# Attention weights of batches 2 and 3 turned on VectorE through DRAM, with a new order on every engine

## The chip, the cores and the metric

One core of one Trainium2 chip runs the program. The metric is device time in microseconds (us), the median of three runs of one kernel. A profile is one more execution, taken by the hardware profiler; its span runs from the first instruction to the last. Engines: PE is TensorE, DVE is VectorE, ACT is ScalarE, POOL is GpSimd, SP is SyncE, which issues every DMA here.

## The reference

Attention over chunks of 32 queries, each against 8 memory keys and a window of at most 56 keys, and behind it a gated feed-forward layer:

```python
# 4 batches, 8 heads, 768 tokens, head size 64; chunk 32, left 16, right 8, 8 memory keys
scores = scale * np.matmul(q_c, k_full.transpose(0, 1, 3, 2))      # k_full: memory keys and window
a = np.exp(scores - max); a = a / (np.sum(a, axis=-1, keepdims=True) + 1e-09)
out[:, :, c_start:c_end] = np.matmul(a, v_full)
# then x = out, tokens x 512
h = np.maximum(x @ w_in, 0.0)                                      # 1024 wide
conv_out = conv_w[0] * h[t - 1] + conv_w[1] * h[t] + conv_w[2] * h[t + 1]
return (h / (1.0 + np.exp(-conv_out))) @ w_out
```

The weights w_in, conv_w and w_out come as float64.

## The kernel before

**Work.** Attention runs in 32 steps, 8 for each batch: half of the tokens (384) by a pair of heads. A step loads q, k and v (L471); PE makes the scores s (L481, 12 fp32 matmuls that the trace shows as 24 records); DVE takes the maximum and subtracts it (L397, L402) or ACT does so inside the exponential (L423); ACT takes exp (L435); DVE sums (L448) and inverts (L455); DVE or POOL normalises (L459). Then PE turns the weights e with three 128x128 matmuls against the identity into a bank t (L502), ACT copies t in two halves into the one block-diagonal tile a_d (L513), and PE multiplies with v into a bank a (L521, 24 records). ACT rounds a into x_hi (L530) and DVE keeps the rest as x_lo (L533). A step's x is a quarter of one half of the feed-forward's input.

**Feed-forward.** Every fp32 product there is three fp32r matmuls, hi by hi, hi by lo, lo by hi. ffn_in (L556) makes h in 16 half rows for each batch, each of 4 quarters by 3 matmuls of 384 columns. The gate takes h through one tap on ACT or DVE (L583, L587), two on DVE (L593), a sigmoid on ACT (L597) and a product on DVE or POOL (L601); split makes g hi on ACT (L611) and g lo on DVE or POOL (L614). ffn_out (L632) makes 6 tiles of 128 tokens for each batch, each of 8 rows of g by 3 matmuls of 512 columns, and ACT copies the bank out (L644). The float64 weights are taken apart into hi and lo by chains of eight or so operations on DVE, ACT and POOL (L289 to L363).

**Two shapes on PE.** Scores and values (L481, L521) use the array in 64x64 pieces, here called tiled; all else uses the whole array. A switch is a change from one to the other.

**Order.** Nothing runs in the order of the code. `Plan` collects operations with a cost, a due number and dependences, and `run` issues them as a list scheduler would, among those ready first the one with the smallest due (L161). Each engine then runs its own list in that fixed order, and an instruction that waits holds up all behind it on its engine; the DMAs stand in one list on SP. The due numbers are straight lines, `lin(name, i)`, out of the table DUE; a switch is charged 12.1 in the choice (L162) and 95 or 120 ns in the cost (L176). Strings such as MULT, LO, NORM and ZADD, one letter for each step or row, say which of V (DVE), G (POOL) and A (ACT) does an operation; in W_IN and W_OUT a small letter puts the first maximum of a weight's chain on POOL (L293).

**PSUM.** Eight banks: two for s, one t, one a, four f, which both ffn_in and ffn_out use.

Of the kernel before, what the change touches and what calls it, by code (L numbers as in the profile page):

```python
# [9 lines left out]
F32 = mybir.dt.float32  # L10
# [12 lines left out]
NH = 2  # L23
# [5 lines left out]
W64 = 4  # L29
# [3 lines left out]
W_IN, W_OUT = "CRScCmcc", "McCCMcmm"  # L33
# [3 lines left out]
TAP = "AAAAAAAAAAAAAAVVAAAAAAAAAVVVVAAA"  # L37
MULT = "VVVGGGGGGVGGGGGGGGVGGVGVVGGGGVVV"
LO = "VGVVVVVGGVVVVVGGVVVGGGGVVVGGVVVV"
SOFT = "VVAVVVVVVVABABAAAVVVVVABBBVVAVAB"  # L40
NORM = "GGGGGGGGVVGGGGGGGGGGGGGGVGVVVGVV"
ZADD = "VGGGGVGGGGGVGGVGGVVVVGGGVGGVVVVV"
GROUP = "11111111"

DUE = {
    "early": (1.3, 2.83), "qk0": (-13.5, 0.8), "v0": (104.5, 0), "late": (-19.1, 0), "w_in": (-14.7, 2.93),
    "w_in_load": (-18.2, 4.91), "w_out": (78.5, 2.37), "w_out_load": (4.1, 15.21), "load": (-130.9, 0),
# [4 lines left out]
    "gate": (29.9, 2.03)  # L52
# [3 lines left out]
class Tile:  # L56


    def __init__(self, ring, make):
        self.ring, self.make, self.t, self.left, self.due = ring, make, None, 0, None  # L60


class Plan:
# [11 lines left out]
    def op(self, eng, cost, due, do, r=(), w=(), shared=False, table=None, mode=None, late=70):  # L75
# [24 lines left out]
        self.ops.append((eng, cost, due, do, after - {i}, tiles, shared, table, mode, late))  # L100
# [10 lines left out]
    def run(self):  # L111
# [13 lines left out]
        free, shared_free, queue_free = defaultdict(float), 0.0, 950.0  # L125
# [9 lines left out]
        for _ in range(n):  # L135
            best = None
            for e, c in cand.items():
                at = []
# [32 lines left out]
            eng, cost, due, do, after, tiles, shared, tab, md, late = ops[i]  # L171
# [42 lines left out]
SWITCH, MODE = 100.2, 12.1  # L214
# [3 lines left out]
def attention_then_gated_ffn(  # L218
# [39 lines left out]
    a_d = const.tile([P, NG * 4, 2, CH], F32, name="a_d")  # L258
    nc.gpsimd.memset(a_d, 0.0)
# [5 lines left out]

    def lin(name, i):
        return DUE[name][0] + DUE[name][1] * i

    def from_f64(src, hi, lo, key, n, kind, due, first):
# [9 lines left out]
        def op(eng, cost, do, r, wr, **kw):  # L281
# [90 lines left out]
    def attention(steps, due, soft, norm, zadd):  # L372


        ns = len(steps)
# [80 lines left out]
        for i, n in enumerate(steps):  # L456
# [17 lines left out]
    def scores(s, q_d, k_t, due):  # L474
# [14 lines left out]
        plan.op("PE", 24 * 30, due, mm, (q_d, k_t), (s,), mode="tiled", late=250)  # L489

    def outcome(n, v_t, e, i, due):
# [3 lines left out]
        t, a = bank("t", 1), bank("a", 1)  # L495
# [4 lines left out]
        def turn():  # L500
            for g in range(NG):
                nc.tensor.transpose(  # L502
                    out=t.t[:, g * P : (g + 1) * P],
                    in_=e.t[:, i, 2 * g : 2 * g + 2].rearrange("p g k -> p (g k)"),
                    identity=ident,
                )
# [294 lines left out]
```

## Time and profile before

| what | value |
| --- | --- |
| time, median of 3 runs (lowest to highest) | 360.23 us (359.33 to 361.78) |
| span of the profiled execution | 357.6 us |
| PE busy | 341.4 us, 95% of the span |
| DVE busy | 244.7 us, 68% |
| ACT busy | 240.4 us, 67% |
| POOL busy | 125.2 us, 35% |
| DMA read, written | 41.84 MB, 6.29 MB |

Matmuls overlap, so a record's length is not what it costs: the step from one start to the next is. A busy share over the whole span mixes stretches with different limits.

### The profile page before, as it was taken

The numbers are of one execution on the slowest core, as the hardware profiler recorded it, in microseconds if no ns is written. First come the engines' busy times: TensorE is split into PE (matmuls) and PEld (weight loads), VectorE is DVE, ScalarE is ACT, GpSimd is POOL, SyncE is SP. The second block draws the span as 40 slices with busy tenths as digits, with TensorE's granted clock in tenths as the row PEclk, the third lists the DMA queues.
The fourth block names the chain that finished last, engine by engine and source line by source line (L and its number), as shares of the span: only waits on it lengthen the run. The fifth ranks groups of instructions, "written<-read, shape, count | busy, mean of one in ns | idle before, by whom it ended". The sixth has DMA issues, their size and how long they took to land.

```text
span 357.6 us, 7589 instructions
## 1 busy us (share of the span) xinstructions
PE 341.4 (95%) x3000; PEld 302.1 (84%) x3000; DVE 244.7 (68%) x408; ACT 240.4 (67%) x492; POOL 125.2 (35%) x167
## 2 busy tenths in 40 slices
PE   1699999999999999999999999999999999999996
PEld 1588899999899987778888899997878799998886
DVE  3899898988889998779933026889644128998000
ACT  4468588878679999887979158877466345675101
POOL 2376554442373253774572003354010002560000
PEclk9989999999999999999999999999999999999999
DMA  7999961969623146134416200006272000000111
GB/s 267 402 387 311 383 234 63 341 208 283 209 95 116 25 139 227 68 104 152 129 44 250 88 31 0 2 0 188 80 294 75 30 31 2 0 0 3 59 59 61
DMA packets 19909, 48.63 MB, mean 136 GB/s; under 512 B 2337, under 2 KB 6689, under 8 KB 19873
## 3 DMA queue, kind: packets, MB, share of 16 engines
q1 hardware_dynamic: 19872, 48.14, 39.0%
q8 instruction: 24, 0.39, 0.5%
q14 instruction: 13, 0.10, 0.1%
HBM read 41.84 MB, written 6.29 MB: 135 GB/s over the span
## 4 chain that ended last, share of the span: by engine, by line
PE 69%; DVE 10%; DMA 5%; ACT 5%; POOL 5%; issue 4%; SPq 1%; POOLq 0%; DVEq 0%; ACTq 0%
PE f L632 33%; PE f L556 24%; PE a L521 5%; PE s L481 5%; DVE c L593 3%; PE t L502 2%; DMA h<-in_k_dram 2%; POOL c L601 2%; DMA w<-in_w_out_dram 2%; ACT c L597 2%; DMA w<-in_w_in_dram 2%; POOL w_top L293 2%; DVE z L448 1%; DVE w_top L299 1%; DVE top L397 1%
## 5 line engine op out<-in xcount | busy, mean ns | idle before, releaser
L632 PE MATMUL f<-w_out_hi,g 128*128 128x512 f32 (+1 forms) x400 | 127.6, 391 | 0.2 <-ACT o_sb L644 0.2
L556 PE MATMUL f<-x_hi,w_in_hi 128*128 128x384 f32 x256 | 88.7, 346 | 0.0
L632 PEld LDWEIGHTS f<-w_out_hi,g 128*128 128x128 f32 x400 | 74.1, 188 | 16.3 <-ACT o_sb L644 0.4
L556 PE MATMUL f<-x_hi,w_in_lo 128*128 128x384 f32 x256 | 86.2, 337 | 0.1
L556 PE MATMUL f<-x_lo,w_in_hi 128*128 128x384 f32 x256 | 86.1, 336 | 0.0
L593 DVE SCALAR_TENSOR_TENSOR c<-h,cw,c 128x768 f32<-128x768 f32 x48 | 65.9, 1380 | 27.6 <-ACT c L583 26.1
L632 PE MATMUL f<-w_out_lo,g 128*128 128x512 f32 (+1 forms) x200 | 77.0, 385 | 0.0
L556 PEld LDWEIGHTS f<-x_hi,w_in_hi 128*128 128x128 f32 x256 | 48.1, 188 | 1.2
L556 PEld LDWEIGHTS f<-x_hi,w_in_lo 128*128 128x128 f32 x256 | 48.2, 188 | 0.5 <-POOL w_in_lo L358 0.4
L556 PEld LDWEIGHTS f<-x_lo,w_in_hi 128*128 128x128 f32 x256 | 48.1, 188 | 0.0
L632 PEld LDWEIGHTS f<-w_out_lo,g 128*128 128x128 f32 x200 | 37.6, 188 | 7.2
L601 POOL TENSOR_TENSOR c<-c,h 128x768 f32<-128x768 f32 x9 | 15.8, 1752 | 70.2 <-ACT c L597 68.1
L459 POOL TENSOR_TENSOR e<-e,z 128x384 f32<-128x384 f32 x24 | 24.9, 1035 | 41.4 <-DVE z L455 27.1
L644 ACT COPY o_sb<-f 128x512 f32<-128x512 f32 (+1 forms) x25 | 14.1, 569 | 35.1 <-PE f L632 32.8
L573 ACT ACTIVATE h<-f 128x384 f32<-128x384 f32 x48 | 23.1, 492 | 17.2 <-PE f L556 16.8
L521 PEld LDWEIGHTS a<-a_d,v_t 128*64 128x64 f32 x768 | 25.7, 140 | 10.3 <-issue 5.0
L513 ACT COPY a_d<-t 64x384 f32<-64x384 f32 x64 | 30.3, 474 | 4.3 <-PE t L502 3.3
L533 DVE TENSOR_TENSOR x_lo<-a,x_hi 128x384 fp32r<-128x384 f32 x32 | 17.6, 551 | 22.3 <-ACT x_hi L530 22.2
L521 PE MATMUL a<-a_d,v_t 128*64 128x64 f32 x768 | 29.9, 229 | 1.9 <-ACT a_d L513 1.8
L597 ACT ACTIVATE c<-c 128x768 f32<-128x768 f32 x32 | 26.9, 845 | 3.8 <-DVE c L593 3.6
L530 ACT CAST x_hi<-a 128x384 fp32r<-128x384 f32 x32 | 15.4, 481 | 20.2 <-PE a L521 18.6
L423 ACT ACTIVATE e<-s,top 128x64 f32<-128x64 f32 (+3 forms) x96 | 24.4, 319 | 4.2 <-DVE top L409 2.8
(73 smaller groups left out, 479.8 us busy)
## 6 DMA issues: line engine op xcount, KB each, us to landing
v_t<-in_v_dram SPq DMA_DIRECT2D x32, 384.0 KB, 4.1
q_d<-in_q_dram SPq DMA_DIRECT2D x28, 384.0 KB, 5.1
k_t<-in_k_dram SPq DMA_DIRECT2D x28, 252.0 KB, 5.2
out_dram<-o_sb SPq DMA_DIRECT2D x23, 256.0 KB, 2.1
w<-in_w_in_dram SPq DMA_DIRECT2D x8, 512.0 KB, 5.9
w<-in_w_out_dram SPq DMA_DIRECT2D x8, 512.0 KB, 6.4
h<-in_q_dram SPq DMA_DIRECT2D x4, 384.0 KB, 7.0
h<-in_k_dram SPq DMA_DIRECT2D x4, 252.0 KB, 7.1
```

What stands on the lines that cost most here:

```text
L423: nc.scalar.activation(part(e, i)[r, g, c], s_()[r, g, c], AF.Exp, bias=part(top, i)[r, g : g + 1], scale=SCALE, accum_out=part(z, i)[r, g ...
L459: lambda i=i: (nc.vector if norm == "V" else nc.gpsimd).tensor_tensor(out=part(e, i), in0=part(e, i), in1=part(z, i).unsqueeze(2).broadcas ...
L481: nc.tensor.matmul(s.t[j * D : (j + 1) * D, o : o + KW], lhsT=q_d.t[:, c], rhs=k_t.t[:, c * STEP : c * STEP + KW], start=True, stop=True,)
L513: nc.scalar.copy(out=a_d[r, :, p, :], in_=t.t[r, : NG * P].rearrange("p (g q) -> p g q", q=CH))
L521: nc.tensor.matmul(a.t[h * D : (h + 1) * D, g * P + j * D : g * P + (j + 1) * D], lhsT=v_t.t[:, g, j, h], rhs=a_d[:, 4 * g + 2 * j + h].re ...
L533: lambda: nc.vector.tensor_tensor(out=x_lo.t[:, cc], in0=a.t[:, :TW], in1=x_hi.t[:, cc].bitcast(F32), op=ALU.subtract),
L556: nc.tensor.matmul(f.t[:, :TW], lhsT=w_in_p[c][:, fc, cc], rhs=x_p[a].t[:, cc], start=(cc == 0 and i == 0), stop=(cc == NCC - 1 and i == 2),)
L573: nc.scalar.activation(h.t[:, 1 + o : 1 + o + TW], f.t[:, :TW], AF.Relu)
L593: lambda i=i: nc.vector.scalar_tensor_tensor(out=c.t, in0=h.t[:, i : i + S], scalar=w[i], in1=c.t, op0=ALU.mult, op1=ALU.add), (*H, c), (c ...
L597: plan.op("A", act(S), due, lambda: nc.scalar.activation(c.t, c.t, AF.Sigmoid), (c,), (c,), table="sigmoid")
L601: lambda: (nc.vector if mult == "V" else nc.gpsimd).tensor_tensor(out=y(), in0=c.t, in1=h.t[:, 1 : S + 1], op=ALU.mult), (c, h), (h if kee ...
L632: nc.tensor.matmul(ps.t[:, :n], lhsT=g[fc][a].t[:, tt * P : (tt + 1) * P], rhs=w_out_p[c][:, fc, o : o + n], start=(fc == 0 and i == 0), s ...
```

## The change

Steps 16 to 31 (batches 2 and 3, the letter B in TURN) no longer use PE and ACT to turn the weights. DVE transposes e in 32x32 blocks into a w64 buffer (L633), two DMAs write the halves to DRAM (L641) and two read them back into place in a block-diagonal tile (L649). Steps 0 to 15 stay as they were. There are two diagonal tiles, a_d0 and a_d1, used in turn, and t and a share a ring of two banks, ta. The output copies use the w_top buffers. Every step and row now has due numbers of its own; the choice charges a switch with 259.41 and the cost with 95 or 245 ns. The strings that place operations are new, and v is laid out on the host to suit.

```diff
-W_IN, W_OUT = "CRScCmcc", "McCCMcmm"
+W_IN, W_OUT = "CRSCCmcr", "mCCCMMCM"
-MULT = "VVVGGGGGGVGGGGGGGGVGGVGVVGGGGVVV"
-LO = "VGVVVVVGGVVVVVGGVVVGGGGVVVGGVVVV"
+MULT = "GVVGGVVVGGVGGVVGVVGVGVVVGVVGGGVV"
+LO = "VVGGGVGGVVVVVVVVGVVVGGVVVVVVVVVV"
-NORM = "GGGGGGGGVVGGGGGGGGGGGGGGVGVVVGVV"
-ZADD = "VGGGGVGGGGGVGGVGGVVVVGGGVGGVVVVV"
+NORM = "GGVGGVVGGVGGGGGVGGVVVGVGVVVVVGVV"
+ZADD = "VVGVVGVGVGVGVVVVVGGVGVVGVGGVVGVG"
+TURN = "PPPPPPPPPPPPPPPPBBBBBBBBBBBBBBBB"
+NA = 2
...
-SWITCH, MODE = 100.2, 12.1
+SWITCH, MODE = 110.35, 259.41
...
-    a_d = const.tile([P, NG * 4, 2, CH], F32, name="a_d")
-    nc.gpsimd.memset(a_d, 0.0)
+    turned = [const.tile([P, 2, 4 * NG, CH], F32, name=f"a_d{i}") for i in range(NA)]
...
-        t, a = bank("t", 1), bank("a", 1)
+        a = bank("ta", 2, DUE["ra"][n])
+        a_d = Tile("a_d", next_turned)
...
+            t = tile_of("w64", W64, [P, WC, 2], U32)
...
+                lambda: nc.vector.transpose(
+                    out=t_().rearrange("p x o q -> p o x q"), in_=e.t[:, i].rearrange("p o (x k) -> p o x k", x=2)
+                ), ((e, i),), (t,),
...
+            d = tile_of("t_dram", 2, [2, 2, 2, CH, W // 2], pool=dram)
+            for x in range(2):
+
+                def away(x=x):
+                    nc.sync.dma_start(
+                        out=d.t[:, :, x].rearrange("j h y n -> (j h) y n"), in_=t_()[:, x].rearrange("p o q -> p (o q)")
+                    )
...
+            for j in range(2):
+
+                def place(j=j):
+                    nc.sync.dma_start(
+                        out=a_d.t[j * D : (j + 1) * D, j].rearrange("p (h o) q -> p h (o q)", h=2),
+                        in_=d.t[j].rearrange("h x y n -> (x y) h n"),
+                    )
...
-        o_sb = tile_of("o_sb", 2, [P, DM])
+        o_sb = tile_of("w_top", 2, [P, WC], U32)
```

Three places in the order show what moves.

PE, before, where batch 3's attention stands among batch 2's outputs (f<-w_out is ffn_out, t the transposes, a the values, s the scores):

```order
L521 MATMUL a<-a_d,v_t 64x64 x12
L502 MATMUL t<-ident,e 128x128 x3
L632 MATMUL f<-w_out_hi,g 128x512
L632 MATMUL f<-w_out_lo,g 128x512
L632 MATMUL f<-w_out_hi,g 128x512 x2
L632 MATMUL f<-w_out_lo,g 128x512
L632 MATMUL f<-w_out_hi,g 128x512
L502 MATMUL t<-ident,e 128x128 x3
```

PE, changed, at the values of batch 3's first two steps (f<-x_hi,w_in is ffn_in of batch 2):

```order
L665 MATMUL ta<-a_d_74,v_t 64x2x32 x12
L665 MATMUL ta<-a_d_73,v_t 64x2x32 x12
L583 MATMUL s<-k_t,q_d 64x64 x24
L694 MATMUL f<-x_hi_2562,w_in_hi 128x384
L694 MATMUL f<-x_hi_2562,w_in_lo 128x384
L694 MATMUL f<-x_lo_2577,w_in_hi 128x384
```

The transposes are gone, and the tiled work of two steps stands together: over the whole program 48 of 96 transposes are left, and 43 switches of 73.

DVE, before, up to the last g lo of batch 0, g_2026 (numbers name buffers):

```order
L533 TENSOR_TENSOR x_lo0_1703<-a_1895,x_hi0_1690 128x384
L402 TENSOR_TENSOR e_1970<-s_1910,top_1962 128x384
L397 TENSOR_REDUCE top_1977<-s_1930 128x6
L402 TENSOR_TENSOR e_1994<-s_1930,top_1977 128x384
L614 TENSOR_TENSOR g_2008<-c_1766,g_1992 128x768
L593 SCALAR_TENSOR_TENSOR c_2001<-g_1117,cw_77,c_2001 128x768
L533 TENSOR_TENSOR x_lo0_1703<-a_1979,x_hi0_1690 128x384
L614 TENSOR_TENSOR g_2026<-c_1853,g_2014 128x768
```

DVE, changed, up to its last g lo of batch 0, g_2007:

```order
L422 SCALAR_TENSOR_TENSOR w64_1777<-w64_1777 128x512
L557 RECIPROCAL z_1892<-z_1892 128x6
L429 TENSOR_SCALAR w64_1777<-w_top_1816 128x512
L671 TENSOR_TENSOR x_lo0_1987<-ta_1918,x_hi0_1954 128x384
L671 TENSOR_TENSOR x_lo0_1987<-ta_1937,x_hi0_1954 128x384
L465 SCALAR_TENSOR_TENSOR w_out_lo_80<-w64_1777 128x512
L633 STREAM_TRANSPOSE w64_2003<-e_1685 128x6x2x32
L752 TENSOR_TENSOR g_2007<-c_1708,g_1867 128x768
```

Ahead of that place DVE now has four transposes and more of the normalising, the maxima and the gate's products, while three of the batch's eight g lo are left to it instead of six.

PE, changed, where it first reads g_2007 (f<-w_out is ffn_out of batch 0; every second g is a hi, the others lo):

```order
L770 MATMUL f_1999<-w_out_hi_79,g_1315 128x512
L770 MATMUL f_1999<-w_out_lo_80,g_1315 128x512
L770 MATMUL f_1999<-w_out_hi_79,g_1349 128x512
L770 MATMUL f_1812<-w_out_hi_79,g_1867 128x512
L770 MATMUL f_1812<-w_out_lo_80,g_1867 128x512
L770 MATMUL f_1812<-w_out_hi_79,g_2007 128x512
```

It is the 39th ffn_out matmul of the list; in the kernel before the corresponding one, which first reads g_2026, is the 57th.

## Rows read from the trace of the kernel before

**Rows 1.** The page's head: span, PE's busy time, granted clock in 40 slices.
```profile
span 357.6 us, 7589 instructions
PE 341.4 (95%) x3000; PEld 302.1 (84%) x3000; DVE 244.7 (68%) x408; ACT 240.4 (67%) x492; POOL 125.2 (35%) x167
PEclk9989999999999999999999999999999999999999
```
**Rows 2.** Busy time by stretch: stretch, length, engines (instructions), PE clock, DMA share, GB/s.
```profile
0.00:20.00 20.00, 9.07 (x140) 7.92 (x142) 13.03 (x34) 10.15 (x22) 7.23 (x15) 0.97 0.93 342
20.00:60.00 40.00, 39.28 (x501) 35.59 (x498) 37.38 (x88) 28.97 (x63) 24.69 (x37) 0.97 0.80 286
60.00:100.00 40.00, 39.28 (x477) 36.34 (x476) 34.80 (x72) 32.96 (x96) 15.00 (x30) 1.00 0.75 244
100.00:140.00 40.00, 39.95 (x371) 36.16 (x371) 37.22 (x61) 36.83 (x62) 17.99 (x17) 1.00 0.37 122
110.00:130.00 20.00, 19.95 (x185) 18.12 (x184) 19.72 (x30) 19.54 (x30) 6.54 (x4) 1.00 0.36 119
190.00:290.00 100.00, 99.71 (x778) 87.34 (x777) 48.17 (x77) 60.45 (x136) 18.00 (x37) 1.00 0.26 89
```
**Rows 3.** PE's waits: who was waited for, us in total, times, longest.
```profile
PE s L481 <- DMA h<-in_k_dram: 8.5, 2, 6.8
PE a L521 <- ACT a_d L513: 1.8, 1, 1.8
```
**Rows 4.** PE in order of time: start, us, what; a transpose and a switch there and back.
```profile
153.83 0.49 PE L502 MATMUL t<-ident,e 128*128 128x128 f32 x3
154.07 0.48 PE L632 MATMUL f<-w_out_hi,g 128*128 128x512 f32 x1
154.39 0.40 PE L632 MATMUL f<-w_out_lo,g 128*128 128x512 f32 x1
...
156.03 0.40 PE L632 MATMUL f<-w_out_hi,g 128*128 128x512 f32 x1
156.35 0.92 PE L521 MATMUL a<-a_d,v_t 128*64 128x64 f32 x24
157.20 0.50 PE L632 MATMUL f<-w_out_hi,g 128*128 128x512 f32 x1
157.54 0.40 PE L632 MATMUL f<-w_out_lo,g 128*128 128x512 f32 x1
```
**Rows 5.** DVE and PE in order of time, where batch 0's last g lo is made and first read.
```profile
138.49 1.01 DVE L593 SCALAR_TENSOR_TENSOR c<-g,cw,c 128x768 f32<-128x768 f32 x1
139.42 0.55 DVE L533 TENSOR_TENSOR x_lo<-a,x_hi 128x384 fp32r<-128x384 f32 x1
139.89 0.94 DVE L614 TENSOR_TENSOR g<-c,g 128x768 fp32r<-128x768 f32 x1
140.75 1.00 DVE L593 SCALAR_TENSOR_TENSOR c<-g,cw,c 128x768 f32<-128x768 f32 x1
...
142.38 0.62 PE L632 MATMUL f<-w_out_hi,g 128*128 128x512 f32 x2
```
**Rows 6.** DVE in order of time, its start.
```profile
4.64 0.43 DVE L315 TENSOR_SCALAR w<-w 128x512 uint32<-128x512 uint32 x1 [4.64 <-DMA w<-in_w_in_dram]
5.11 0.69 DVE L320 SCALAR_TENSOR_TENSOR w<-w 128x512 uint32<-128x512 uint32 x1
```
**Rows 7.** DVE by line and form: busy us, mean ns, idle before.
```profile
L593 DVE SCALAR_TENSOR_TENSOR c<-h,cw,c 128x768 f32<-128x768 f32 x48 | 65.9, 1380 | 27.6 <-ACT c L583 26.1
L459 DVE TENSOR_TENSOR e<-e,z 128x384 f32<-128x384 f32 x8 | 4.4, 556 | 0.2
```
**Rows 8.** DMA issues (KB each, us to landing) and the SP queue's waits.
```profile
q_d<-in_q_dram SPq DMA_DIRECT2D x28, 384.0 KB, 5.1
out_dram<-o_sb SPq DMA_DIRECT2D x2, 128.0 KB, 1.7
...
SPq L471 <- PE a L521: 132.3, 24, 37.2
```

More of the change, by code (lines that the diff above doesn't have):

```diff
@@ L99, in op @@
             x.due = due if x.due is None else x.due
-        self.ops.append((eng, cost, due, do, after - {i}, tiles, shared, table, mode, late))
+        self.ops.append((eng, cost, due, do, after - {i}, tiles, shared, table, mode, late, gap))
         return i
@@ L170, in run @@
             t, e, i = best
-            eng, cost, due, do, after, tiles, shared, tab, md, late = ops[i]
+            eng, cost, due, do, after, tiles, shared, tab, md, late, gap = ops[i]
             if tab and tab != table:
@@ L175, in run @@
             if md and md != mode:
-                cost += 95 if md == "tiled" else 120
+                cost += CHANGE[mode, md]
                 mode = md
+            if e == "PE" and t < COLD:
+                cost *= 2
             if e == "DMA":
                 queue_free = max(queue_free, t + 600) + cost
-                end, free[e] = queue_free + 1400, t + 60
+                end, free[e] = queue_free + 1400, t + gap
             else:
@@ L184, in run @@
                     shared_free = t + (cost * 0.78 if e == "G" else cost - 120)
-                end = free[e] = t + cost
+                end = t + cost
+                free[e] = end - LESS.get(e, 0)
             cand[e].remove(i)
@@ L200, in run @@
         return max(x[1] for x in self.times)
+CHANGE = {(None, "whole"): 0, (None, "tiled"): 0, ("whole", "tiled"): 95, ("tiled", "whole"): 245}
+COLD = 16000
+LESS = {"V": 80, "A": 100, "G": 40}
+WAIT = 300
 def vec(n, rate=1, ptr=0):
@@ L462, in attention @@
             )
-            outcome(n, v_of[n], e, i, due)
+            outcome(n, v_of[n], e, i)
     def load(tile, src, due, flat=None):
@@ L529, in outcome @@
-        plan.op("PE", 24 * 30, due + DUE["late"][1], values, (v_t, ("a_d", 0), ("a_d", 1)), (a,), mode="tiled", late=250)
+                        r = slice(h * D, (h + 1) * D)
+                        if TURN[n] == "P":
+                            o, y = (2 * u + h) * NG + g, a.t[r, g * P + u * D : g * P + (u + 1) * D]
+                        else:
+                            o, y = h * 6 + 2 * g + u, a.t[r, g * P : (g + 1) * P].rearrange("p (j u q) -> p u j q", j=2, u=2)[:, u]
+                        nc.tensor.matmul(y, lhsT=v_t.t[:, g, u, h], rhs=a_d.t[:, :, o], start=True, stop=True)
@@ L530, in outcome @@
+        plan.op("PE", 700, sum_due, values, (v_t, (a_d, 0), (a_d, 1)), (a,), mode="tiled", late=250)
         plan.op("A", act(TW, True), due, lambda: nc.scalar.copy(out=x_hi.t[:, cc], in_=a.t[:, :TW]), (a,), ((x_hi, cc),))
@@ L680, in attention_then_gated_ffn, with tokens_out, splits @@
+    def tokens_out(b, g, tiles, last=False):
+        for tt in tiles:
+            start, each = DUE["out"][6 * b + tt], DUE["os"][6 * b + tt]
+            ffn_out(b, g, tt, [start + each * fc for fc in range(NFC)], 2 if last and tt == 5 else 1)
+    def splits(b, y):
+        return [split(*y[fc], DUE["split"][b * NFC + fc], LO[b * NFC + fc]) for fc in range(NFC)]
     steps(0, 4)
     for fc in range(NFC):
-        convert("in", w_in[fc], w_in_p, fc, W_IN[fc], lin("w_in", fc), lin("w_in_load", fc))
@@ L702, in attention_then_gated_ffn @@
-    steps(16, 24)
-    t = DUE["out"][0]
-    def out_rest(b, g, t, last):
-        for tt in range(3):
-            ffn_out(b, g, tt, [t + 2.1 * fc + 0.1 * tt for fc in range(NFC)])
-        for tt in range(3, 6):
-            ffn_out(b, g, tt, [t + 17 + 5.7 * (tt - 3) + 0.7 * fc for fc in range(NFC)], 2 if last and tt == 5 else 1)
-    out_rest(1, g, t, False)
-    t += 34 + 8
+        convert("out", w_out[fc * P : (fc + 1) * P], w_out_p, fc, W_OUT[fc], DUE["w"][NFC + fc], DUE["wl"][NFC + fc])
```

257 lines of the change are left out of this document (176 added, 81 removed), and 10 rows, old and new, of the table DUE.

## The prediction

> **What bounds the kernel now.** I read first how much of the span PE fills, then what PE waited for, then the stretches. PE is busy for 341.4 of 357.6 us, and its clock is granted at nearly full rate, except for two slices of the first thirty us [rows 1]. Its waits add up to little more than 10 us, and 8.5 of them are for the first loads [rows 3]. By stretches PE has under 0.8 us of idle time in each 40 us from 20 to 100 us, and after that almost none [rows 2]. So the end is set by the sum of what PE has to do, and an engine beside it counts where it keeps PE waiting. The second thing to see is which engine comes nearest to that: DVE is busy for 13.0, 37.4, 34.8 and 37.2 us of the first 20, 40, 40 and 40 us, that is 122.4 of 140, but for only 48.2 of the 100 us from 190 to 290 [rows 2]. And it is just in time: the last g lo of batch 0 is done at 140.83 us and PE reads it at 142.38 [rows 5]. Up to there DVE has no slack, after about 190 us it has plenty.
>
> **What PE gains.** The 48 transposes of batches 2 and 3 go, in 16 groups of three. A group moves the next matmul on by 154.07 - 153.83 = 0.24 us, and that one's step is 0.32 instead of 0.23 us: 0.33 us together [rows 4], times 16 is 5.3 us. The two copies on ACT for each of these steps go too; they cost nothing off the path. Switches fall from 73 to 43. There and back costs 0.09 us (156.03 to 156.35 instead of 0.23), 0.15 (24 records take 0.85, in the middle of a tiled run 0.70) and 0.11 (157.20 to 157.54): 0.35 us for a pair [rows 4], times 15 is 5.2 us. The matmuls of ffn_in now alternate with those of ffn_out; both use the whole array, so I charge nothing, and a hidden price there would be the same kind of step as in rows 4, 0.1 us in the worst case, 59 times, 6 us. PE alone would thus end 10.5 us earlier: 357.6 - 10.5 = 347.1 us of span.
>
> **What DVE has to do first.** I follow the DVE list up to the last g lo of batch 0 that it makes, in both orders. Counting one step from start to start when nothing is in the way (0.93 us for 768 columns by three operands, 0.86 for g lo and products, 0.47 for 384 columns [rows 5]; 0.60 for 512 columns by three operands [rows 6]; the plain 512-column ones, 0.43 long, at 0.34, since a step is about 0.08 us less than a length, as 1.01 and 0.93 show), the list before comes to 15 x 0.93 + 9 x 0.86 + 75 x 0.47 + 41 for the weights + 5 for small ones = 103 us. It finished at 140.83. Of the 37.8 us between, 17.6 are idle (140 - 122.4, rows 2), and some 20 are instructions drawn out: the two-tap operation takes 1.01 us alone and 1.38 on average [rows 5, 7].
>
> The list after holds to the same place: 4 more weight maxima (+1.4), one chain of the weights' shift and join less (-0.9), one subtraction, two sums, five normalisings of 384 columns more and one x_lo less (+3.3), one tap and two products more (+2.6), three g lo less (-2.6), four transposes, and 9 small ones (+0.8). A 32x32 transpose on DVE is in no row of before; from below it costs a 384-column step of 0.47, from above twice a 384-column instruction, 1.1 us [rows 7]. I take 0.47, as the same elements pass once: +1.9 us, at worst +4.4. The sum is +6.5 us.
>
> Drawing out goes by what POOL does: 20 us against 64.9 us of POOL's busy time up to 140 us [rows 2], 0.30 us for each. By the letters POOL has some 9 us less up to there (five normalisings, seven small sums, four maxima and two products less, three g lo and one weight more), so DVE gets 0.30 x 9 = 2.7 us back. The row shows stretching while POOL works; the Trainium skill ("SBUF — State Buffer", section "SBUF: two separate sides") says that POOL shares one port pair with DVE's instructions that read two SBUF inputs, as an exclusive lock in which the loser waits for the whole instruction. By that rule read at its hardest, all 9 us would come back, and the end would fall to PE's own sum; the trace agrees in direction only, with its 0.30.
>
> What is left is the idle time. 7.0 of the 17.6 us lie in the first 20 [rows 2], where DVE waits 4.64 us for the first load [rows 6] and then for scores; the changed SP list begins with the same three transfers, so they stay. The other 10.6 us come where DVE waits now and then for scores, for POOL, for ACT or for a load. In 110:130, where it is the engine that PE hangs on, it is idle for 0.28 of 20 us [rows 2]. With two banks ta and two diagonal tiles a step's values wait less for the step before, and PE now reaches the place with less work behind it, so it runs ahead and DVE rarely waits for it. I take that rate, 1.7 us over 120 us, so 8.9 us are saved; the bounds are none saved and all 10.6.
>
> Batch 0's last g lo is then done at 140.8 + 6.5 - 2.7 - 8.9 = 135.7 us. Can PE be there first? It has 39 instead of 57 ffn_out matmuls ahead of the place, 366 instead of 384 of ffn_in, four groups of transposes less and 29 instead of 49 switches; that is 12 us less, 130.4 us at today's waits. So PE waits there for some 5 us. Behind the place PE has 18 matmuls of 0.233 us and 18 of 0.173 us more, 12 groups of transposes and 10 switches less: 4.2 + 3.1 - 4.0 - 1.7 = +1.6 us on the 215.2 us that it needed from 142.38 to 357.6 [rows 1, 5]. The end is 135.7 + 0.2 + 215.2 + 1.6 = 352.7 us of span.
>
> **The way through DRAM.** No row of before writes DRAM and reads it back. A store of 128 KB lands 1.7 us after its issue, a 384 KB load under traffic 5.1 us [rows 8]; a round trip of two stores and two loads of 96 KB each is between twice 1.7 and twice 5.1 us, and I take 8 with the issues. The steps where it is closest are 16 and 17: between the transpose of step 17 and the x_lo that needs it, DVE has 15 us of other work, and in later pairs 35 us and more. So it hides. The stores stand in the one SP list, behind loads that wait for PE, where one such wait was 37.2 us long [rows 8]; the loads ahead of these stores wait for tiles that were free long before.
>
> **Rivals.** *PE-paced*: each microsecond that POOL gives up brings DVE nearly a whole one instead of 0.30, or drawing out falls to two thirds of today's rate, and g lo is there by 130.4 us. Then only the 10.5 us count: 347.1 us. For it speaks that DVE's drawn-out time is the least certain term; against it that DVE's own 109.5 us, 7 of start and 15 of drawing out already make 131.5. *DVE keeps its idle time*: all 10.6 us stay, because what it waits for (ACT's roundings, scores, loads) is still late. Then g lo is done at 144.6 us and the end is 361.6: slower than before; it decides once more than 6 of the 10.6 us stay. *The round trip is late*: at steps 16 and 17 a store queues behind a load on SP that waits for a value group of PE. The cover is 15 us; a hold-up of 20 us costs 5 on top of the sum, 358, of 25 us 363. It needs a wait such as the 37.2 us one to stand ahead of exactly this store.
>
> **How the numbers follow.** The profiled span lies 2.6 us below the median of 360.23, and I add that to each: DVE-paced 355.3 us, PE-paced 349.7, DVE idle as before 364.2, round trip late 361 to 366. Chances: DVE-paced 0.50 (of its own range, 352.5 to 359.5, a bit over half is below 356.6), PE-paced 0.25, idle as before 0.15, late trip 0.10. What a measurement of this kernel can tell from no change is about 1%, 3.6 us. Faster by more than that: 0.30 + 0.25 = 0.55; within it: 0.20 from the first, half of the third and a part of the fourth, 0.32; slower: 0.13. The range that leaves out 2 in 10 runs from 349 to 364.
>
> **What would show it.** Right: PE's idle time before 140 us grows by about 5 us, put down to DVE's g lo or x_lo; DVE is busy for over 95% of 20 to 135 us; transposes take 0.5 to 0.6 us; from 190 us on PE has no gaps, and its starts across a change of ffn_in and ffn_out keep 0.17 and 0.23 us. Wrong: PE waits for a_d tiles or their DMAs; DVE's gaps before 140 us stay near 17 us; the two-tap operations fall well below 1.38 us, which would mean that POOL's part was worth more than 0.30.

## The result, and the profile after

The changed kernel takes 354.25 us (median of 4 runs, 353.96 to 354.79) against 360.74 us for the kernel before in the same group (359.33 to 361.78): a ratio of 0.983, 95% interval 0.980 to 0.986. The forecast was 355.3 us, between 349 and 364. Timed once more beside other kernels it took 354.46 us, 0.982 (0.977 to 0.987).

The head of the page of the changed kernel: busy time of each engine with its number of instructions, then PE's granted clock in 40 slices of the span. It answers to [rows 1].

```profile
span 351.8 us, 7516 instructions
PE 333.7 (95%) x2952; PEld 297.3 (84%) x2952; DVE 248.3 (71%) x454; ACT 220.2 (63%) x442; POOL 94.8 (27%) x143
PEclk9999999999999999999999999999999999999999
```

PE is as full as before (95%), with 48 instructions less; the clock is granted in every slice. By stretches (columns: length, then busy time and number of instructions of PE, PEld, DVE, ACT and POOL, PE clock, DMA share and GB/s), to be read against [rows 2]:

```profile
20.00:60.00 40.00, 38.76 (x548) 35.28 (x545) 36.46 (x100) 31.85 (x82) 22.07 (x32) 1.00 0.93 323
60.00:100.00 40.00, 39.38 (x420) 36.84 (x419) 39.49 (x80) 38.91 (x91) 9.20 (x21) 1.00 0.56 188
100.00:140.00 40.00, 38.33 (x394) 34.16 (x393) 39.45 (x72) 31.52 (x47) 19.98 (x22) 1.00 0.58 189
190.00:290.00 100.00, 100.00 (x870) 90.69 (x869) 52.59 (x93) 51.57 (x106) 13.03 (x31) 1.00 0.39 122
```

DVE is now full from 60 to 140 us (78.9 of 80 us; 72.0 before), and ACT with it from 60 to 100. PE's idle time has moved to 20 to 140 us, where it is 3.5 us (1.5 before); from 190 us on it has none. What PE waited for (sum, times, longest), against [rows 3]:

```profile
PE s L583 <- DMA h<-in_k_dram: 9.7, 4, 6.4
PE f L770 <- DVE g L752: 2.3, 2, 1.7
PE ta L611 <- POOL e L561: 0.9, 1, 0.9
PE ta L665 <- DVE x_lo L671: 0.5, 1, 0.5
```

No line of the whole list names t_dram or a load of a_d, so the way through DRAM is hidden; its one line on a_d, 0.3 us, is for ACT's copy at 30.7 us, in a step that is still turned on PE. The longest wait behind the start is the forecast one, at batch 0's last g lo. The timeline of DVE, of POOL and of PE there (start, duration, and in brackets the idle time ahead and its releaser):

```profile
130.78 2.23 DVE L465 SCALAR_TENSOR_TENSOR w_out_lo<-w 128x512 fp32r<-128x512 uint32 x1
132.94 0.56 DVE L633 STREAM_TRANSPOSE w<-e 128x384 f32<-128x384 f32 x1
133.43 0.91 DVE L752 TENSOR_TENSOR g<-c,g 128x768 fp32r<-128x768 f32 x1
```
```profile
130.63 1.84 POOL L752 TENSOR_TENSOR g<-c,g 128x768 fp32r<-128x768 f32 x1
```
```profile
134.39 0.50 PE L770 MATMUL f<-w_out_hi,g 128*128 128x512 f32 x1 [1.67 <-DVE g L752]
```

g lo is done at 134.34 us (forecast: 135.7) and PE waits 1.7 us for it (forecast: 5).

**Where the 5.8 us between the two spans went.** I add up the step that each matmul has when nothing is in the way, take 0.165 us for each of the switches that the trace shows (a little under half of the 0.35 that [rows 4] give for a pair), and call the rest waiting:

| us | before | after | difference |
|---|---|---|---|
| up to the first matmul | 6.8 | 6.4 | -0.4 |
| matmuls and transposes at their steps | 322.6 | 317.4 | -5.2 |
| switches, 73 and 43 | 12.0 | 7.1 | -5.0 |
| waiting, up to 20 us | 8.0 | 8.9 | +0.9 |
| waiting, 20 to 60 us | 2.6 | 3.4 | +0.8 |
| waiting, 60 to 110 us | 1.2 | 2.1 | +0.9 |
| waiting, 110 to 170 us | 0.5 | 3.1 | +2.6 |
| waiting behind 170 us, and the tail | 3.8 | 3.4 | -0.4 |

PE has 10.2 us less to do and waits about 5 us more: the two terms of the forecast, 10.5 and 5. But only 2.6 of the 5 us lie around the two last g lo; the rest is spread over the first 110 us.

One part of the table's "waiting" is not waiting. In the kernel before, PE's clock was granted at 0.50 (the lower of its two levels, 1.2 GHz) from 18.8 to 22.2 us, after a start in which PE had been busy for less than half of the time [rows 2]; the changed kernel has the full clock throughout.

```profile
18.80:22.20 3.40, 3.00 (x50) 2.84 (x50) 3.34 (x7) 1.79 (x5) 3.24 (x4) 0.50 1.04 399
```

The matmuls of that stretch make some 1.5 us at their steps and kept PE busy for 3.0, so this cost about 1 us or a little more (an estimate). So about 1 us of the 5.8 comes from the clock and not from the change of PE's work, and the waits proper grew by about 6 us.

### The profile page after: what moved, and what is told of

It is laid out like the page before. It is cut to its first block, busy times and chain, and to the rows that moved or that the text cites. A ratio compares the mean times of both kernels' runs of the same rounds, so it can differ in the third digit from the quotient of the medians.

```text
span 351.8 us, 7516 instructions
## 1 busy us (share of the span) xinstructions
PE 333.7 (95%) x2952; PEld 297.3 (84%) x2952; DVE 248.3 (71%) x454; ACT 220.2 (63%) x442; POOL 94.8 (27%) x143
## 4 chain that ended last, share of the span: by engine, by line
PE 71%; DVE 16%; DMA 7%; ACT 3%; issue 1%; SPq 1%; POOL 1%; DVEq 0%; ACTq 0%
PE f L770 31%; PE f L694 30%; PE ta L665 5%; DVE c L731 5%; DMA w<-in_w_in_dram 4%; PE s L583 4%; DMA h<-in_k_dram 2%; DVE top L511 1%; DVE x_lo L671 1%; DVE top L499 1%; DVE g L752 1%; DVE w L417 1%; DVE w L422 1%; DVE z L550 1%; DVE w_top L408 1%
## 5 line engine op out<-in xcount | busy, mean ns | idle before, releaser
L770 PEld LDWEIGHTS f<-w_out_hi,g 128*128 128x128 f32 x400 | 74.0, 188 | 18.5 <-DVE g L752 3.2
L731 DVE SCALAR_TENSOR_TENSOR c<-h,cw,c 128x768 f32<-128x768 f32 x48 | 49.7, 1054 | 11.0 <-ACT c L721 10.3
L671 DVE TENSOR_TENSOR x_lo<-ta,x_hi 128x384 fp32r<-128x384 f32 x32 | 17.2, 549 | 40.3 <-ACT x_hi L668 39.5
L782 ACT COPY w_top<-f 128x512 f32<-128x512 f32 (+1 forms) x25 | 14.1, 573 | 36.4 <-PE f L770 29.3
L739 POOL TENSOR_TENSOR c<-c,h 128x768 f32<-128x768 f32 x6 | 10.9, 1829 | 79.3 <-ACT c L735 79.3
L665 PEld LDWEIGHTS ta<-a_d,v_t 128*64 128x64 f32 x768 | 25.4, 143 | 4.4 <-issue 3.0
L665 PE MATMUL ta<-a_d,v_t 128*64 128x64 f32 x768 | 27.9, 230 | 0.8 <-DVE x_lo L671 0.5
L583 PE MATMUL s<-k_t,q_d 128*64 128x64 f32 x672 | 23.7, 223 | 0.5 <-DMA k_t<-in_k_dram 0.5
L583 PEld LDWEIGHTS s<-k_t,q_d 128*64 128x64 f32 x672 | 21.5, 138 | 2.8 <-issue 2.6
L749 ACT CAST g<-c 128x768 fp32r<-128x768 f32 x24 | 19.5, 831 | 6.3 <-DVE c L739 3.3
L752 DVE TENSOR_TENSOR g<-c,g 128x768 fp32r<-128x768 f32 x16 | 17.3, 1088 | 6.4 <-ACT g L749 6.2
```

The source lines that it names most:

```text
L583: nc.tensor.matmul(s.t[j * D : (j + 1) * D, o : o + KW], lhsT=q_d.t[:, c], rhs=k_t.t[:, c * STEP : c * STEP + KW], start=True, stop=True,)
L665: nc.tensor.matmul(y, lhsT=v_t.t[:, g, u, h], rhs=a_d.t[:, :, o], start=True, stop=True)
L671: lambda: nc.vector.tensor_tensor(out=x_lo.t[:, cc], in0=a.t[:, :TW], in1=x_hi.t[:, cc].bitcast(F32), op=ALU.subtract),
L731: lambda i=i: nc.vector.scalar_tensor_tensor(out=c.t, in0=h.t[:, i : i + S], scalar=w[i], in1=c.t, op0=ALU.mult, op1=ALU.add), (*H, c), (c ...
L739: lambda: (nc.vector if mult == "V" else nc.gpsimd).tensor_tensor(out=y(), in0=c.t, in1=h.t[:, 1 : S + 1], op=ALU.mult), (c, h), (h if kee ...
L749: plan.op("A", act(S), due, lambda: nc.scalar.copy(out=g_hi(), in_=x()), (h,), (p[0],))
```

## Experiments

In several of these the arrival of the first loads differs from run to run: the pair of value groups that the list puts near 54 us begins at 53.7 to 56.1 us in kernels that are the same up to there. So I also give the time from that pair (24 matmuls, ta<-a_d,v_t) to PE's first read of batch 0's last g lo, "the middle stretch", and the time from that read to the end. In the changed kernel they are 134.39 - 53.74 = 80.65 and 351.78 - 134.39 = 217.39 us (80.52 and 217.37 in the second run). Runs 2, 3 and 6 have the same list up to the place; their middle stretches are 80.64, 80.67 and 80.61 us. So it is steady to within 0.2 us, wherever the pair begins. The pair's row:

```profile
53.74 0.92 PE L665 MATMUL ta<-a_d,v_t 128*64 128x64 f32 x24
```

**1 and 2: DVE longer, early or late.** In the lambda of x_lo, with (0, 8) and with (24, 32):

```diff
+            for _ in range(3 if 0 <= n < 8 else 1):
+                nc.vector.tensor_tensor(out=x_lo.t[:, cc], in0=a.t[:, :TW], in1=x_hi.t[:, cc].bitcast(F32), op=ALU.subtract)
```

> The changed kernel in its own order, with each x_lo subtraction of batch 0 (steps 0 to 7) made three times instead of once: 16 more instructions of DVE between 20 and about 100 us, a step of 0.48 us each, 7.7 us. Theory (DVE paces PE up to the last g lo of batch 0 and of batch 1): g lo is done some 6 to 7.7 us later than at 134.3 us, and the end moves with it, 354.3 to about 360.5 us (359.5 to 362). Rival (PE's own sum paces the kernel, DVE's gaps before 140 us take the extra work up): the end moves by less than 2 us, 354 to 356.

Measured: 363.24 us, 1.009 (1.006 to 1.012). The read at the place comes at 144.23 us instead of 135.09, and from there to the end it is 217.39 us as ever. A repeated x_lo follows after 0.59 us, not 0.48 (three take 1.73 us, below), so 9.4 us were added, and the end comes 9.1 us later in the profiled execution. Of that, 0.6 may be the loads (the first matmul starts at 7.17 instead of 6.53 us) and about 1 the clock, granted at 0.50 from 27.2 to 30.6 us; in the two executions with the full clock the span is 8.1 us longer than the mean of the second run of the changed kernel. PE's waits show that they come in at many places, not at one:

```profile
PE f L694 <- DVE x_lo L671: 2.4, 2, 1.2
PE f L770 <- DVE g L752: 2.3, 2, 1.6
PE ta L611 <- DVE x_lo L671: 2.1, 2, 2.0
```

The wait for g lo itself is no longer than before, since PE arrives as late as DVE. Adding to DVE early costs most of the amount. The test has a weakness: the repeats also make x_lo itself late, a tile that PE waits for, so it does not separate a longer list on DVE from a later hand-over of this one tile (the waits of 2.4 and 2.1 us).

> The same 16 extra subtractions, but in batch 3 (steps 24 to 31), that is behind 200 us, where DVE is busy for about half of the time. Theory (DVE paces nothing there): 354.3 us as without them, within 1 us, and no new wait of PE behind 190 us. Rival (DVE's lateness counts wherever it is added): 360 to 362 us as with the early ones.

Measured: 361.31 us, 1.005 (1.002 to 1.007). The theory falls: up to the place nothing changes (135.60 us), but from there to the end it takes 223.30 us, 5.9 more of the 9.4. PE's waits, DVE's timeline around 264 us, and DVE and PE at 290 us:

```profile
PE f L770 <- DVE g L752: 3.2, 3, 1.7
PE f L694 <- ACT w_top L782: 1.5, 1, 1.5
```
```profile
261.83 1.95 DVE L752 TENSOR_TENSOR g<-c,g 128x768 fp32r<-128x768 f32 x1 [1.64 <-ACT g L749]
263.71 1.73 DVE L671 TENSOR_TENSOR x_lo<-ta,x_hi 128x384 fp32r<-128x384 f32 x3
265.35 0.95 DVE L752 TENSOR_TENSOR g<-c,g 128x768 fp32r<-128x768 f32 x1
...
288.16 3.39 DVE L671 TENSOR_TENSOR x_lo<-ta,x_hi 128x384 fp32r<-128x384 f32 x6 [14.02 <-ACT x_hi L668]
```
```profile
291.61 0.44 PE L694 MATMUL f<-x_lo,w_in_hi 128*128 128x384 f32 x1 [1.35 <-DVE x_lo L671]
```

DVE is busy for half of the time from 190 to 290 us, but not evenly: from 235 to 255 us it is 94% full (18.73 of 20 us), and at 264 us g lo stands behind the x_lo that were lengthened. Yet a full DVE is not needed for a loss: at 290 us PE waits 1.35 us for an x_lo although DVE had been idle for 14.0 us ahead of it, since its input came no earlier and PE wants the tile at once. Half idle on average is not slack at a given place.

**3: the transposes back on PE.** Ahead of the first matmul of ffn_in for the second halves of batches 2 and 3:

```diff
             def mm(cc=cc):
+                if b >= 2 and hf == 1 and cc == 0:
+                    for g in range(NG):
+                        nc.tensor.transpose(out=f.t[:, g * P : (g + 1) * P], in_=ident, identity=ident)
```

> The changed kernel in its own order, with 16 groups of three 128x128 transposes put back on PE, between matmuls of ffn_in that use the whole array, in batches 2 and 3 (their output is overwritten by the matmuls that follow). Theory (PE has no slack behind 165 us, and a group costs 0.33 us): +5.3 us, 359.5 us (358.5 to 360.5). Rival (what the transposes cost beside ffn matmuls is hidden, and the gain came from the order alone): 354.3 us, within 1 us.

Measured: 360.83 us, 1.003 (1.001 to 1.005). From the place to the end 222.79 us: 5.4 us more, 0.34 us for a group of three. The first term of the sum, 0.33 us, holds.

**4: the old price for a switch.**

```diff
-SWITCH, MODE = 110.35, 259.41
+SWITCH, MODE = 110.35, 12.1
```

> One part of the change undone: the planner's price for a switch between whole-array and 64x64 matmuls is 12.1 again instead of 259.41. The list then has 71 switches on PE instead of 43: 8 pairs more ahead of the first read of batch 0's last g lo, 6 pairs more behind it. Theory (PE waits for DVE ahead of that place, so only pairs behind it count, 0.33 us each): +2.0 us, 356.3 us (355.3 to 357.5), unless the other order delays DVE. Rival (each pair counts): +4.7 us, 359.0 us. Second rival (switches are hidden behind weight loads): 354.3 us.

Measured: 383.18 us (380.33 to 386.91), 1.062 (1.054 to 1.071); all three expectations fall. The profiled execution has 81 switches, not 71: 38 more at 0.165 us are 6.3 of the 31 us. The rest, 25, is waiting and what follows from it, and the largest part of that is the rival of the late round trip, which the changed kernel itself never shows (PE's wait first, then what stands around the longer one on the timelines of DVE, PE and SP, and PE behind it by engines and clock):

```profile
PE ta L665 <- DMA a_d<-t_dram: 12.1, 2, 10.3
```
```profile
304.59 1.04 DVE L633 STREAM_TRANSPOSE w<-e 128x384 f32<-128x384 f32 x2
```
```profile
315.18 1.12 PE L665 MATMUL ta<-a_d,v_t 128*64 128x64 f32 x16 [10.25 <-DMA a_d<-t_dram]
```
```profile
305.19 2.33 SPq L641 DMA_DIRECT2D t_dram<-w  x4
309.68 3.36 SPq L649 DMA_DIRECT2D a_d<-t_dram  x4
```
```profile
315.20:322.40 7.20, 6.63 (x60) 6.35 (x61) 1.12 (x2) 1.45 (x3) 0.00 (x0) 0.50 0.01 2
```

With this price the planner puts the last two transposes of batch 3 just ahead of their values. The first ends at 305.17 us, 0.58 after its start, and its values start at 315.18: the way through DRAM is 10.0 us long when SP issues at once and no other load stands ahead. The stores are issued over 2.3 us, the loads go out some 2 us behind the last of them, and issuing the four takes another 3.4 us. I had taken 8, for one step's two stores and two loads; here two steps share the way, and no run shows one alone.

A wait of this kind costs more than its own length. The clock fell to 0.50 during it, at 308.8 us, and stayed there until 322.5: a matmul of ffn_in then steps by 0.32 instead of 0.17 us. It was at 0.50 for 23.9 us in three stretches of this execution, and by the steps some 6 of the 25 us are PE at that clock (an estimate). The due times were made for one price; with another they give a list that is late in many places, so this run says little of what a switch costs.

**5 and 6: the changed kernel again, and switches forced into its own order.**

> The changed kernel as it is, to stand beside the others of this group on the same chip: 354.3 us (353.5 to 355.5).

Measured: 354.46 us, as above.

```diff
             def mm(cc=cc):
+                if b >= 2 and cc == 0:
+                    nc.tensor.matmul(f.t[:D, :D], lhsT=ident[:, :D], rhs=ident[:, :D], start=True, stop=True)
```

> The changed kernel in its own order, with 32 single matmuls of a 128x64 tile by 64 columns put between the whole-array matmuls of ffn_in in batches 2 and 3 (their output is overwritten): 32 pairs of switches more on PE. Theory (PE paces behind 165 us, a pair costs 0.33 us, the matmul itself 0.03): +11.5 us, 365.8 us (364 to 368). Rival (the smaller number of switches in the changed kernel is worth nothing, since the weight loads hide them): +1 us, 355.3 us.

Measured: 369.66 us, 1.023 (1.018 to 1.029). From the place to the end 231.66 us, 14.3 more, 0.45 us for each. The page counts 3016 matmuls, 64 more and not 32, so each is two passes of 0.03 us, 1.9 us together. The trace shows 103 switches, 60 more than in the changed kernel, since some of these matmuls stand right behind tiled ones: 30 pairs. That leaves 0.41 us for a pair, a little above the 0.35 of the forecast. Fifteen pairs are worth 5.0 us by the table above and 6.2 by this.

**7: less of POOL.** The normalisings of steps 0 to 15, maxima, products and sums of the weights and gate products of batches 0 and 1, where POOL makes them, over 64 columns, as in

```diff
-                lambda: G.tensor_tensor(out=ftop(), in0=ftop(), in1=fbits(), op=ALU.add), (x, U), (x,), shared=True,
+                lambda: G.tensor_tensor(out=ftop()[:, :64], in0=ftop()[:, :64], in1=fbits()[:, :64], op=ALU.add), (x, U), (x,), shared=True,
```

> The changed kernel in its own order, with POOL's work up to batch 0's last g lo cut: its normalisings of steps 0 to 15, maxima and products of the weights, and products of batches 0 and 1 run over 64 columns only, so the results are left partly undone. POOL's busy time up to 134 us falls from 61.5 to about 36 us. Theory (DVE paces PE there, and each us of POOL draws DVE out by 0.23 us): DVE gets 5.8 us back, PE's waits for g lo at 134 and 164 us vanish and the end falls to PE's own sum, by 2.7 to 5 us: 349.3 to 351.6 us; the two-tap operations of DVE before 134 us get shorter than their 1.09 us. Rival (DVE is drawn out by DMA traffic or by PSUM, not by POOL): their length stays, and the end moves by less than 1 us. Second rival (PE is held by something else): shorter operations, the same end.

Measured: 353.70 us, 0.980 (0.974 to 0.986). Busy times, and the two-tap operation up to 134 us (columns: number, busy time, mean ns):

```profile
PE 332.1 (95%) x2952; PEld 297.2 (85%) x2952; DVE 241.3 (69%) x454; ACT 220.2 (63%) x442; POOL 69.3 (20%) x143
```
```profile
L731 DVE SCALAR_TENSOR_TENSOR c<-g,cw,c 128x768 f32<-128x768 f32 x16 | 17.6, 1104 | 0.1
```

25.5 us less of POOL give DVE 7.0 us back over the span, 0.27 for each: the rate of the forecast (0.30) is about right. But the middle stretch is shorter by only 0.8 us (79.74 against 80.52) and the end by another 0.8 behind it. The two-tap operations before 134 us are as long as they were (1.097 us in the changed kernel), against my expectation: thirteen of the 16 take their 1.0 us in both kernels, and the other three (1.83, 1.47 and 1.20 us, from 109.8 to 115.7 us) begin while POOL is at a g lo or at the normalising of a later step, which this kernel kept. Of the 25.5 us, 13.6 were cut before 60 us, where PE waits for loads of k_t, and 7.4 behind 134 us.

**8: a version meant to be faster**, with PE's order kept: the convolution's weights first, two g lo of batch 0 on POOL, four first taps of batch 1 on ACT.

```diff
+        queue = nc.scalar if key == "cw2" else nc.sync
...
-            lambda: (nc.vector if lo == "V" else nc.gpsimd).tensor_tensor(
+            lambda: (nc.vector if lo == "V" and due not in TO_POOL else nc.gpsimd).tensor_tensor(
...
+                lambda: nc.scalar.activation(c.t, h.t[:, 0:S], AF.Copy, scale=w[0]) if due in TO_ACT
```

> A version meant to be faster, with PE's order kept: the small chain on the convolution's weights runs first, on a load from ACT's queue, while DVE waits for the first large load (some 1.0 us less of DVE work behind it); two g lo of batch 0 go from DVE to POOL where POOL is idle (81 and 87 us; 0.86 us each less, 0.48 us of it given back as drawing out); four first taps of batch 1 go from DVE to ACT (2.1 us less, behind 134 us). Theory (DVE paces PE up to 164 us): PE's two waits for g lo, 1.8 and 0.8 us, shrink by 1.8 to 2.6 us in sum, 351.7 to 352.5 us. Rival (ACT, busy for 38.9 of the 40 us from 60 to 100, or POOL, is as late as DVE): no gain, 354.3 us or more.

Measured: 358.58 us, 0.995 (0.992 to 0.998): 4 us slower than the changed kernel, the rival's side. PE's waits, and DVE's timeline beside the two g lo that POOL now makes (1.89 us from 82.34 and 2.33 from 86.41):

```profile
PE f L784 <- DVE g L766: 3.1, 2, 1.7
PE ta L624 <- POOL e L574: 2.8, 1, 2.8
PE ta L624 <- DVE x_lo L684: 1.3, 2, 1.1
```
```profile
82.89 1.75 DVE L408 TENSOR_SCALAR w_top<-w_top 128x512 f32<-128x512 f32 x1 [0.37 <-ACT w_top L404]
...
86.96 2.07 DVE L408 TENSOR_SCALAR w_top<-w_top 128x512 f32<-128x512 f32 x1
```

None of the three moves paid. The 24 KB load was there only after 5 us, and everything on DVE stood behind it (PE waits 2.8 us for the first normalising, against 0.9). The two g lo on POOL were 1.7 us less for DVE and took back 3.0: two operations that take 0.42 us alone took 1.75 and 2.07 while POOL was at them, and not the 0.48 in all that I had expected. The value groups near 54 us then began on time again (54.80 us), since PE waits for loads before them anyway. In the middle stretch (82.06 us) 1.5 us were lost, 1.1 of them at 97 us, where PE waits for an x_lo of DVE; another 2.0 behind it, where PE waits for g of batch 1 from ACT (0.6 us) and DVE.

**9, 10 and 11: DVE shorter, ACT shorter, both.** The two-tap operations of batch 0 over their last 384 columns; its sigmoids over 64 columns; both.

```diff
-                    out=c.t, in0=h.t[:, i : i + S], scalar=w[i], in1=c.t, op0=ALU.mult, op1=ALU.add
+                    out=c.t[:, cut:], in0=h.t[:, i + cut : i + S], scalar=w[i], in1=c.t[:, cut:], op0=ALU.mult, op1=ALU.add
...
-        plan.op("A", act(S), due, lambda: nc.scalar.activation(c.t, c.t, AF.Sigmoid), (c,), (c,), table="sigmoid")
+        m = 64 if due in BATCH0 else S
+        plan.op("A", act(S), due, lambda: nc.scalar.activation(c.t[:, :m], c.t[:, :m], AF.Sigmoid), (c,), (c,), table="sigmoid")
```

> The changed kernel in its own order; the 16 two-tap operations of batch 0 on DVE (64 to 125 us) run over the last 384 of their 768 columns only, so half of the convolution is left out. That takes 16 x 0.40 = 6.4 us from DVE ahead of the last g lo of batch 0. Theory (from 55 to 134 us DVE alone paces PE): PE's wait of 1.7 us at the place, and with it 0.8 us at batch 1's, vanish, 351.8 to 352.6 us instead of 354.4. Rival (DVE and ACT are both full there, ACT with 39 of the 40 us from 60 to 100, so that one alone gives little back): 353.5 to 354.5 us, and DVE shows idle time put down to ACT.

> The changed kernel in its own order; the eight sigmoids of batch 0 on ACT (72 to 127 us) run over 64 of 768 columns only, the rest is left out: 8 x 0.6 = 4.8 us less of ACT, DVE's work as it was. Theory (DVE alone paces): 354.4 us, within 0.7 us. Rival (both are full): 353 to 354 us, the wait at the place shorter by up to 1 us.

> Both cuts of the two kernels before together. Theory (DVE alone paces): as with DVE's cut alone, 351.8 to 352.6 us. Rival (both are full): clearly less than with either alone, 351.5 to 352.5 us against 353.5 or more.

Measured: 354.65 (0.984, 0.977 to 0.990), 355.35 (0.986, 0.982 to 0.991) and 353.23 us (0.983, 0.978 to 0.988): the times alone decide nothing, since the value groups began 0.8 to 1.5 us later than in the second run of the changed kernel. The middle stretch decides: 79.04, 80.29 and 78.36 us against 80.52, that is 1.5, 0.2 and 2.2 us less. In the kernel with DVE shorter, the two-tap operations up to 136 us, the engines by stretches, and what DVE waited for between 60 and 134 us:

```profile
L731 DVE SCALAR_TENSOR_TENSOR c<-g,cw,c 128x384 f32<-128x384 f32 x16 | 10.9, 686 | 0.0
```
```profile
60.00:100.00 40.00, 39.93 (x426) 37.55 (x425) 38.31 (x83) 39.44 (x91) 9.56 (x23) 1.00 0.61 202
100.00:134.00 34.00, 33.85 (x376) 30.87 (x374) 31.24 (x59) 28.62 (x46) 19.93 (x23) 1.00 0.57 185
```
```profile
DVE x_lo L671 <- ACT x_hi L668: 1.0, 3, 0.4
```

The 16 operations take 10.9 us instead of 17.5, 6.6 us less, and 1.5 us arrive. DVE now waits for ACT (2.6 us in several lines between 60 and 134 us, 0.3 in the changed kernel; 0.7 more for POOL), and PE is idle for 0.2 of 74 us up to 134. So DVE did pace PE, but only by some two microseconds: behind that PE has hardly any idle time left, and its own sum decides. ACT alone is worth nothing measurable here, with DVE's cut another 0.7 us. At the place PE still waits 0.8 us for g lo; what made that g lo late I cannot put down to one engine.

**12: the turn back on PE.**

```diff
-TURN = "PPPPPPPPPPPPPPPPBBBBBBBBBBBBBBBB"
+TURN = "PPPPPPPPPPPPPPPPPPPPPPPPPPPPPPPP"
...
+    for n in rank:
+        DUE["rt"][n], DUE["p"][n] = DUE["ra"][n] - 0.02, DUE["ra"][n] - 0.01
```

> One part of the change undone: all steps turn their weights on PE again, into the shared banks, with ACT's copies; no way through DRAM, no transposes on DVE. The order of batches 0 and 1 is the same up to step 16, behind it the list is planned anew (the due times of steps 16 to 31 for the banks and the values' loads are put in the order of their softmax), with 57 switches instead of 43. Theory (PE has no slack behind 165 us): 16 groups x 0.33 us = +5.3 us, 5 to 7 pairs of switches at 0.39 us = +2 to +2.7 us, and 1 us back at batch 0's last g lo since DVE has three transposes less ahead of it: 360 to 362 us. Rival (the turn on PE costs nothing beside its own matmuls, the order made the gain): 354 to 356 us.

Measured: 380.60 us, 1.057 (1.053 to 1.061). The page has the 48 matmuls again (5.2 us) and 57 switches (2.3 us); the span is longer by 26, and about 18 of that is new waiting, some 4 us of it PE at a granted clock of 0.50 (an estimate from the steps; 13.7 us at 0.50 in three stretches). The largest waits behind the start are 4.9 us for ACT's copies into a_d, 3.2 for loads of k_t and 2.9 for ACT's e.

As in run 4, one letter was changed under due times that were made for the other. What the turn on DVE is worth with due times made for the turn on PE stays open; the 5.4 us of run 3 are its cost on PE alone.

## Why the prediction was right, and where it was not

**PE's sum.** Right, term by term: 0.34 us for a group of transposes (0.33 forecast, run 3), 0.41 us for a pair of switches (0.35, run 6), 10.2 us together by the table (10.5), which takes the switch at a price near the forecast's. The clock was passed over: the row shows one lower slice, not two, and about 1 us was gained because the changed kernel has none. Changing between ffn_in and ffn_out costs nothing, as charged: in the changed kernel the steps across the change are 0.23 us behind an ffn_out matmul and 0.17 behind one of ffn_in.

```profile
130.63 0.39 PE L770 MATMUL f<-w_out_hi,g 128*128 128x512 f32 x1
130.86 0.34 PE L694 MATMUL f<-x_hi,w_in_hi 128*128 128x384 f32 x1
...
131.22 0.34 PE L694 MATMUL f<-x_lo,w_in_hi 128*128 128x384 f32 x1
131.39 0.40 PE L770 MATMUL f<-w_out_hi,g 128*128 128x512 f32 x1
```

**DVE up to the place.** Right in sum: the g lo is done at 134.3 us instead of 135.7. If its own work is the 109.5 us of the forecast, then of the other 24.8, 10.0 are idle (8.7 forecast), and 14.8 are drawn out (17.3 forecast), against 61.5 us of POOL, 0.24 for each:

```profile
0.00:134.30 134.30, 120.21 (x1460) 109.75 (x1460) 124.29 (x275) 107.32 (x229) 61.49 (x90) 1.00 0.74 256
```

POOL had not 9 us less up to there, but about 3 (61.5 at 134 us, 64.9 at 140 before), so the give-back that I counted on was mostly not there, and a lower rate than I took made up for it: at 0.30 the 61.5 us would have drawn DVE out by 18.5 us. That the two errors cancel is luck. A transpose on DVE steps by 0.49 to 0.50 us (0.47 taken; the mean length of the 16 is 0.565).

**PE's wait at the place.** The step that failed in its form: "PE waits there for some 5 us". It waits 1.7 there and 0.7 at batch 1's last g lo. I let PE run to the place at "today's waits", there by 130.4 us, and so put all of DVE's lateness into one wait. PE was there at 132.7: it had waited 2.6 us more in the first 110 us than the kernel before, and g lo came 1.4 us earlier than forecast. What made PE late on its way is not settled. A pacing engine can hand its lateness over at each tile that PE takes from it, and run 1 shows that, with its 9 us spread over waits for x_lo, for g lo and for other tiles of DVE; but in the changed kernel the list of waits puts only 0.5 us ahead of the place to a tile of DVE, and most of the 2.6 us is in pieces too small for it. The sum stayed right because the time of g lo, not the wait, sets what follows: from the place to the end it is 217.4 us (216.8 forecast).

**DVE paces up to 140 us.** Half right. Lengthening it costs most of the amount (some 8 of 9.4 us, run 1, with the weakness named there), shortening it gains little (1.5 of 6.6, run 9), since PE's own sum and ACT follow within two microseconds. The rival of a PE-paced kernel, 349.7 us, needed all of the lateness to go; no run reached it, the least being 353.2 us.

**"After about 190 us it has plenty".** Wrong: 9.4 us added there cost 5.9 (run 2). I read slack from a mean over 100 us, but DVE's tiles come just in time there too: behind other work at 264 us, behind a late input at 290.

**The way through DRAM.** Hidden, as said, with 13.6 us between the end of step 17's transpose (113.73 us) and its values (127.34). Its length may have been too small at 8: for two steps at once it is 10.0 us (run 4). The rival was a real one: with another list it cost 10.3 us in one place.

**The two-tap operation.** I wrote that a mean well below 1.38 us would mean that POOL's part was worth more than 0.30. The same 48 now take 1.05 on average, and POOL's part is not worth more. The 1.38 [rows 7] were the mean of the 48 operations of batches 1 to 3, which all start behind 141 us. Those of batch 0, ahead of the place, had 1.14 up to 140 us and have 1.10; they carried only some 2 of the 20 us that I called drawn out (15 times 0.13). Behind 170 us it was 1.41 and is 1.07, where PE waits for none of the gate's tiles in either kernel. The lines of the kernel before up to 140 us and behind 170 us, and of the changed one for the same stretches:

```profile
L593 DVE SCALAR_TENSOR_TENSOR c<-g,cw,c 128x768 f32<-128x768 f32 x15 | 17.0, 1141 | 0.9 <-ACT c L583 0.8
...
L593 DVE SCALAR_TENSOR_TENSOR c<-h,cw,c 128x768 f32<-128x768 f32 x37 | 51.9, 1412 | 26.7 <-ACT c L583 25.3
```
```profile
L731 DVE SCALAR_TENSOR_TENSOR c<-g,cw,c 128x768 f32<-128x768 f32 x16 | 17.5, 1097 | 0.0
...
L731 DVE SCALAR_TENSOR_TENSOR c<-h,cw,c 128x768 f32<-128x768 f32 x32 | 33.6, 1070 | 10.9 <-ACT c L721 10.3
```

## What to carry to other kernels

Where PE is full, count what it no longer has to do (and look at its granted clock on both sides), and set against it when the engine that feeds it finishes its list; the time of the last hand-over is worth more trust than where the waits will show. In a balanced list, price both directions: here a microsecond more on the second engine cost most of a microsecond, and one less gained only what separated it from PE's own sum and the third engine. Read slack and durations from the stretch in question, not from a mean over the span, and don't judge one part of a planned order by switching it back under due times that were made for the whole: runs 4 and 12 lost 26 to 31 us that way.

## What was unexpected of the hardware

POOL holds DVE for a whole instruction in places: DVE's 512-column operation of 0.68 us took 2.23 us beside a g lo of 1.84 us on POOL (at 130.78 us, shown above). That agrees with the lock that the Trainium skill describes ("SBUF — State Buffer", section "SBUF: two separate sides"), and yet the mean over all of POOL's work is only 0.24 to 0.27 us for each of its microseconds. One reason is on the timeline: where DVE began first it kept its 1.01 us, and POOL's g lo was the longer, 2.31 us instead of 1.84. In run 8 an operation with one input was held as well: 0.42 us alone, 2.07 beside a g lo on POOL.

```profile
120.24 1.01 DVE L731 SCALAR_TENSOR_TENSOR c<-g,cw,c 128x768 f32<-128x768 f32 x1
```
```profile
120.66 2.31 POOL L752 TENSOR_TENSOR g<-c,g 128x768 fp32r<-128x768 f32 x1 [5.70 <-ACT g L749]
```

A repeated x_lo that overwrites the same tile follows after 0.59 us instead of 0.48: in the trace of run 1 each repeat waits for DVE's own semaphore, which the first one does not. So a test made of repetitions adds more than its share: 9.4 us where I had counted 7.7.

PE's clock can turn a wait into a longer loss: it fell to 0.50 in the 10.3 us wait of run 4 and kept PE at half speed for 7.3 us behind it.
